# Output projection of three token blocks, head by head over both column halves, and Wo loaded in eight pieces

## The chip, the cores and the metric

The kernel runs on one core of a Trainium2 chip, as one launch. The metric is the device time of an execution in microseconds (us). Each kernel's time is the median of several executions; one more execution was recorded by the hardware profiler, and its trace is what the tables below come from.

## The reference

Two independent layers are computed on sequences of 2048 tokens of width 1024, and their outputs are set side by side. The first is a state-space layer (a complex diagonal recurrence over time with input and output matrices). The second, which the change concerns, is an attention with memory: 64 segments of 32 tokens, each preceded by 8 memory rows, 32 heads of width 128.

```python
for s in range(n_seg):
    xs = x[:, s * seg_len:(s + 1) * seg_len, :].copy()
    h = jnp.concatenate([mem, xs], axis=1)
    q, k, v = (jnp.einsum('btd,dhe->bhte', h, W) for W in (Wq, Wk, Wv))
    scores = jnp.where(mask, jnp.einsum('bhqe,bhke->bhqk', q, k) * scale, -1e9)
    o = jnp.einsum('bhqk,bhke->bhqe', softmax(scores), v)
    o = jnp.einsum('bhte,hed->btd', o, Wo)      # the output projection
    mem = o[:, :M, :].copy()
    outs.append(o[:, M:, :])
```

(Here the three projections and the mask are put on one line each.) The output projection is, for each token, a sum over 32 heads x 128 values against Wo, which has 1024 columns.

## The kernel before

**Stages.** Stage 1 interleaves the state-space layer's first products with the value projection. Stage 2 is the state-space output. Then come the query and key projections, interleaved with attention for 16 head pairs; the memory rows are guessed ahead, so that all segments run at once. The last stage is the output projection, with a range and tolerance check of the guess inside it (`check`). If the check fails, a flag sends the kernel into a slow general loop (`general`), which is not executed here.

**The output projection.** Attention stores its results in DRAM (`b_on`). Transposing DMAs on SP's queue bring them back as `ol[h]`, one tile of 128 (head width) x 512 tokens for each head; in the trace they are called b_ol. There are four blocks of 512 tokens (`tb`), each with four tiles of 128 tokens (`tt`). A matmul has 128 tokens of `ol[h]` as its stationary operand and 512 columns of Wo as the moving one. 32 such matmuls, one for each head, add up in one PSUM bank to a tile of 128 x 512. Wo lies in SBUF as two halves: `wo0` (columns 0 to 511; it takes over a buffer named t32, and the trace calls it t) and `wo1` (columns 512 to 1023; wo in the trace).

- `outproj_first` does block 0. Parts of it run between the last attention steps.
- `outproj` does blocks 1 to 3: for each `tt` and each half, 32 matmuls (`out_mm`) and then the eviction (`out_fin`): the vector engine (DVE) copies half 0 into the output tile b_ost, ScalarE (ACT) half 1, and SP stores the tile.
- `out_last` does the last tile of all in three parts of 512, 256 and 256 columns, each with its own copy and store, so that little is left behind the last matmul.

**PSUM.** Eight banks: three for tag "P" (trace: psP), two for "S" (psS), two for "O", one for "R" (psR). In blocks 1 to 3 before the change only "P" and, for the check, "R" are used.

**The check.** It is a generator of five steps. The first step loads b_omT; the other four are called by `next(ck, None)` each time `outproj` yields in block 2: two groups of 128 matmuls on psP (one for each half of Wo), a DVE reduction to c_ss, and last the flag. The flag step has two matmul groups on psR: the first sums c_ss over partitions, DVE then works out c_t, c_ok and c_bad from it, and the second (`ones` against c_bad) gives the flag, which DVE turns into an integer.

**Order.** A scheduler sets the order of instructions on each engine, except where `tc.keep_in_program_order` or the set `k.pin` holds it. With "PE" in `k.pin`, every call through `k.PE` keeps its program order; that is the case in stage 1 and 2 and, at the end, in block 3. `hint` places a branch hint on PE that must stand ahead of the branch to the general loop. DMA issues stand in their engine's queue (SP's for nearly all of the ones here) in order, and an issue that waits holds up those behind it.

Every matmul in this kernel is recorded through the same helper line (L69), so the profile is read by tile names.

Of the kernel before, what the change touches and what calls it, by code (L numbers as in the profile page):

```python
# [25 lines left out]
H = 32; E = 128; SEG = 32; M = 8; NSEG = 64; L = M + SEG  # L26
# [49 lines left out]
class K:  # L76
# [11 lines left out]
    def ps(self, tag, shape=(128, 512), dt=FP32):  # L88
        pool = self.psp if tag in "PR" else self.psx
        return pool.tile(list(shape), dt, name="ps" + tag, bufs={"P": 3, "S": 2, "R": 1, "O": 2, "U": 2}[tag])  # L90

    def copy(self, e, out, in_):
        if e == "s":
            self.S.activation(out, in_, ACT.Copy)  # L94
        else:
            self.V.tensor_copy(out, in_)  # L96
# [256 lines left out]
class PartB:  # L353
# [461 lines left out]
    def out_last(self, ol):  # L815

        k = self.k
        ot = self.p4a.tile([128, D], BF16, name="b_ost", bufs=4)
        for i, (c0, c1) in enumerate(((0, 512), (512, 768), (768, 1024))):
            p = k.ps("P")  # L820
            for h in range(H):
                k.PE.matmul(p[:, 0:c1 - c0], ol[h][:, 384:512], self.wo[c0 // 512][:, h, c0 % 512:c0 % 512 + c1 - c0], start=(h == 0), stop=(h == H - 1))
            k.copy("vsv"[i], ot[:, c0:c1], p[:, 0:c1 - c0])
            k.SP.dma_start(self.out[0, T - 128:T, D + c0:D + c1], ot[:, c0:c1])
            yield

    def outproj(self, tb, ol):
        k = self.k
        osts = {}
        for tt in range(4):  # L830
            if 4 * tb + tt == TT - 1:
                yield from self.out_last(ol)
                return
            for half in range(2):
                p = k.ps("P")
                self.out_mm(p, ol, tt, half, 0, H)
                self.out_fin(p, tb, tt, half, osts)
                yield


    def check(self):
# [166 lines left out]
def hint(k):  # L1008

    k.tc.mark_branch_hint_location("general", "LikelyTaken", engines=[mybir.EngineType.PE])  # L1010
    i = k.nc.cur_bb.bb.instructions[-1]
    k.tc.keep_in_program_order(type("Ins", (), {"ins": i}))


def kernel_main(tc, A_x, A_Lre, A_Lim, A_Bre, A_Bim, A_Cre, A_Cim, A_logdt, A_Dskip, B_x, B_mem0, B_Wq, B_Wk, B_Wv, B_Wo, out,
                force=False, dbg=None):
    with ExitStack() as ctx:
        k = K(tc, ctx)
# [3 lines left out]
        b = PartB(k, B_x, B_mem0, B_Wq, B_Wk, B_Wv, B_Wo, out)  # L1022

        def pool(name, side, bufs=2):
            return tc.tile_pool(name=name, bufs=bufs, side=side, reuse_waits="tile")
# [8 lines left out]
        with pool("p1x", "right") as p1x, pool("p1", "right", 1) as p1:  # L1034
# [29 lines left out]
            for kind, pc, q in order[1:]:  # L1064
# [3 lines left out]
                if kind == "v":  # L1068
                    b.v_x(pc, q, wv[pc])
                    if q == 3:  # L1070
                        if pc >= 3:
                            b.og(pc, wv[pc])
                        n = (pc + 2) if pc + 2 < PC else (2, 0)[pc + 2 - PC]
# [3 lines left out]
                n = 4 * pc + q  # L1077
# [27 lines left out]
        with pool("p2h", "right") as p2h, pool("p2", "right") as p2:  # L1105
# [5 lines left out]
            for i, _ in enumerate(s2):  # L1111
                if i in (1, 4, 7):
                    n = (2, 0, 1)[(i - 1) // 3]
# [25 lines left out]
        wo0 = t32.tile([128, H, 512], BF16, name="t32")  # L1139
# [6 lines left out]
        first, b.ol0 = None, []  # L1146
        for n, (hp, u) in enumerate(at):
            if n == 12:
                k.SP.dma_start(wo0[:], b.Wo[:, :, 0:512])
            if hp % 2 == 0 and 2 < hp + 2 < HP:  # L1150
                if u == 4:
                    vm = b.v_mem(hp // 2 + 1)
                if u in (4, 6, 8):
                    next(vm)
            if hp == 13 and u in (3, 6, 9):
                b.load_o_early(u // 3 - 1)
            want = min(18 * HP, LEAD + (n + 1) * 18 // 11)
            while done < want:
                next(pr)
                done += 1  # L1160
            if done == 18 * HP:
                if first is None:
                    xs.close()
                    b.p4a = ctx.enter_context(pool("p4a", "left", 1))
                    wo1 = b.p4a.tile([128, H, 512], BF16, name="wo1")
                    b.wo = (wo0, wo1)
                    b.load_o_early(3)
                    for h in range(0, H, 16):
                        k.SP.dma_start(wo1[:, h:h + 16, :], b.Wo[:, h:h + 16, 512:D])
                    first = b.outproj_first()  # L1170
                next(first)
                next(first)
# [2 lines left out]

        with pool("p4", "left") as p4:
            b.p4 = p4
            ol = b.load_o_all(1)
            for _ in first:
                pass  # L1180
            for tb in range(1, 4):
                nx = b.load_o_all(tb + 1) if tb < 3 else None
                if tb == 3:
                    k.pin.add("PE")
                if tb == 1:
                    ck = b.check()
                    next(ck)
                for n, _ in enumerate(b.outproj(tb, ol)):
                    if tb == 3 and n == 4:
                        hint(k)  # L1190
                    if tb == 2:
                        next(ck, None)
                ol = nx
# [9 lines left out]
@with_exitstack  # L1203
def kernel(
    ctx: ExitStack,
    tc: tile.TileContext,
    A_x: bass.AP,
    A_Lambda_re: bass.AP,
    A_Lambda_im: bass.AP,
    A_B_re: bass.AP,  # L1210
    A_B_im: bass.AP,
    A_C_re: bass.AP,
    A_C_im: bass.AP,
    A_log_dt: bass.AP,
    A_Dskip: bass.AP,
    B_x: bass.AP,
    B_mem0: bass.AP,
    B_Wq: bass.AP,
    B_Wk: bass.AP,
    B_Wv: bass.AP,  # L1220
    B_Wo: bass.AP,
    B_seg_len: bass.AP,
    out: bass.AP,
):
    assert int(B_seg_len) == SEG
    kernel_main(tc, A_x, A_Lambda_re, A_Lambda_im, A_B_re, A_B_im, A_C_re, A_C_im, A_log_dt, A_Dskip,
                B_x, B_mem0, B_Wq, B_Wk, B_Wv, B_Wo, out)
# [35 lines left out]
```

## Time and profile before

| | |
|---|---|
| time, median of 4 executions | 1238.62 us (1238.37 to 1238.72) |
| profiled execution: time / span | 1238.27 us / 1236.6 us |
| PE busy | 1229.9 us, 8174 matmuls and as many weight loads |
| DVE / ACT / POOL busy | 680.7 / 266.5 / 271.1 us |
| DMA | 174.20 MB, mean 141 GB/s |
| granted TensorE clock | 1.000 |
| blocks 1 to 3 of the output projection on PE | 1057.79 to 1232.35 us |
| last DVE copy | 1232.38 us, 0.42 us long |
| Wo issues on SP | first half at 511.00 us; second half at 999.89 and 1011.15 us |

The span runs from the first to the last recorded instruction; the execution's own time has 1.7 us more. "Busy" of PE counts matmuls with modelled ends: a matmul of 512 columns is shown as 0.38 us long, but the next one starts 0.216 us after it, so rows of a group are read from start to start. In the views below a line of the timeline has the start, the length of the group, engine, line, operation, output <- inputs, shape and count, and in square brackets the idle time before it with what ended it. In the list of waits a line has the waiter, what it waited for, the total, the number of times and the longest.

### The profile page before, as it was taken

How to read it: one execution, taken by the hardware profiler on the slowest of the kernel's cores; microseconds unless marked ns; L12 is line 12 of the kernel's file. 1: busy time of each engine (PE TensorE's matmuls, PEld its weight loads, DVE VectorE, ACT ScalarE, POOL GpSimd, SP SyncE). 2: the span in 40 equal slices, each digit the busy share in tenths (PEclk: the TensorE clock that was granted, in tenths of full speed). 3: DMA queues.
4: the chain of work that ended last, by engine and by line, in shares of the span. 5: the costliest groups of instructions: out<-in, count | busy, mean ns of one | idle time of the engine just before them, and what ended most of it. 6: DMA issues, size and time to landing. Idle time of an engine off the chain costs nothing.

```text
span 1236.6 us, 20043 instructions
## 1 busy us (share of the span) xinstructions
PE 1229.9 (99%) x8174; PEld 654.3 (53%) x8174; DVE 680.7 (55%) x1270; ACT 266.5 (22%) x694; POOL 271.1 (22%) x437
## 2 busy tenths in 40 slices
PE   9999999999999999999999999999999999999998
PEld 4444444444455555556666656555665554445444
DVE  4799999998711124666666666666666641001000
ACT  4444444443310000211112211111221110000000
POOL 4111232112322321322222222323222320000000
PEclk9999999999999999999999999999999999999999
DMA  9943455562898834855464645546574279507000
GB/s 243 249 148 93 126 142 141 155 171 88 232 301 265 248 120 95 228 132 139 96 154 109 153 109 130 131 91 132 116 151 96 61 208 241 108 17 154 18 17 27
DMA packets 321268, 174.20 MB, mean 141 GB/s; under 512 B 145882, under 2 KB 308876, under 8 KB 321172
## 3 DMA queue, kind: packets, MB, share of 16 engines
q1 hardware_dynamic: 299076, 145.33, 48.9%
q10 hardware_dynamic: 21072, 24.38, 6.0%
q0 software_dynamic: 1024, 3.17, 0.7%
q8 instruction: 65, 1.06, 0.4%
q14 instruction: 31, 0.25, 0.1%
HBM read 84.42 MB, written 53.96 MB: 112 GB/s over the span
## 4 chain that ended last, share of the span: by engine, by line
PE 98%; SPq 1%; DMA 0%; DVE 0%; issue 0%
PE psP L69 83%; PE psU L69 9%; PE psS L69 3%; PE psO L69 2%; PE psR L69 1%; SPq L69 1%; DMA b_wv<-in_B_Wv_dram 0%; DVE b_ost L96 0%
## 5 line engine op out<-in xcount | busy, mean ns | idle before, releaser
L69 PE MATMUL psP<-b_xe,b_wk 128*128 128x480 bf16 (+1 forms) x1280 | 247.5, 343 | 0.0
L69 PE MATMUL psP<-b_xe,b_wq 128*128 128x480 bf16 (+1 forms) x1280 | 247.5, 343 | 0.0
L69 PE MATMUL psP<-b_wv,b_xe 128*128 128x512 bf16 (+2 forms) x1048 | 224.5, 372 | 0.1
L689 POOL TENSOR_TENSOR b_m<-b_e,maskB 99x396 bf16<-99x396 bf16 (+1 forms) x160 | 134.4, 840 | 335.7 <-ACT b_e L688 335.7
L688 ACT ACTIVATE b_e<-psS 99x396 bf16<-99x396 f32 (+3 forms) x208 | 91.5, 442 | 530.4 <-PE psS L69 530.4
L69 PEld LDWEIGHTS <-b_wk 128*128 128x128 bf16 x1280 | 119.2, 98 | 94.2
L69 PEld LDWEIGHTS <-b_xe 128*128 128x128 bf16 x1056 | 101.8, 98 | 119.5 <-DMA b_xe<-in_B_x_dram 0.4
L69 PEld LDWEIGHTS <-b_wq 128*128 128x128 bf16 x1280 | 118.5, 98 | 87.7
L96 DVE CAST b_k<-psP 128x480 bf16<-128x480 f32 (+1 forms) x192 | 97.3, 528 | 100.0 <-PE psP L69 100.0
L96 DVE CAST b_q<-psP 128x480 bf16<-128x480 f32 (+1 forms) x192 | 97.3, 528 | 92.2 <-PE psP L69 90.9
L69 PEld LDWEIGHTS <-b_ol 128*128 128x128 bf16 x864 | 84.3, 98 | 94.4
L69 PE MATMUL psU<-a_xT,a_bt 128*128 128x512 bf16 x512 | 114.8, 379 | 0.0
L69 PE MATMUL psP<-t,a_hl 128*128 128x512 bf16 x512 | 113.1, 379 | 0.0
L96 DVE CAST b_ost<-psP 128x512 bf16<-128x512 f32 (+1 forms) x17 | 11.5, 676 | 177.6 <-PE psP L69 177.6
L69 PE MATMUL psP<-wo,b_ol 128*128 128x512 bf16 (+1 forms) x448 | 92.5, 364 | 0.0
L69 PE MATMUL psP<-t,b_ol 128*128 128x512 bf16 x416 | 92.2, 379 | 0.0
L94 ACT ACTIVATE b_vst<-psP 128x512 bf16<-128x512 f32 x126 | 72.3, 589 | 76.9 <-PE psP L69 72.8
L289 POOL TENSOR_SCALAR a_tt<-a_pr,a_tabf 128x1 f32<-128x1 f32 x48 | 34.6, 721 | 245.7 <-DVE a_pr L284 245.7
L706 DVE TENSOR_TENSOR b_ob<-psO,b_accR 99x384 bf16<-99x384 f32 x160 | 86.0, 554 | 2.9 <-DVE b_accR L705 0.4
L69 PEld LDWEIGHTS <-a_bt 128*128 128x128 bf16 x512 | 49.8, 98 | 59.5
L69 PEld LDWEIGHTS <-a_hl 128*128 128x128 bf16 x512 | 49.1, 98 | 56.6
L274 DVE TENSOR_TENSOR a_pr<-psU,a_tabf 128x2048 f32<-128x2048 f32 x32 | 73.1, 2284 | 9.2 <-PE psU L69 9.1
(203 smaller groups left out, 967.4 us busy)
## 6 DMA issues: line engine op xcount, KB each, us to landing
b_v<-b_vx SPq DMA_DIRECT2D x16, 1122.0 KB
b_wv<-in_B_Wv_dram SPq DMA_DIRECT2D x16, 1024.0 KB
b_vx<-b_vst ACTq DMA_DIRECT2D x24, 544.0 KB
b_on<-b_ob SPq DMA_DIRECT2D x15, 720.0 KB
a_hs<-a_h SPq DMA_DIRECT2D x32, 256.0 KB
b_wog<-in_B_Wo_dram SPq DMA_DIRECT2D x4, 2048.0 KB
b_wq<-in_B_Wq_dram SPq DMA_DIRECT2D x16, 512.0 KB
b_wk<-in_B_Wk_dram SPq DMA_DIRECT2D x16, 512.0 KB
```

The lines of the kernel that those rows point to most:

```text
L69: r = f(*a, **kw)
L94: self.S.activation(out, in_, ACT.Copy)
L96: self.V.tensor_copy(out, in_)
L274: V.tensor_tensor(pr[:], u[:].unsqueeze(1).to_broadcast([128, 2, 2, TB]), view(t3, [[TB + 1, 2], [TB + 1, 2], [1, TB]]), ALU.mult)
L289: G.tensor_scalar(tt[:, j:j + 1], w[:, j, TB - 1:TB], t3[:, 1, TB:TB + 1], None, ALU.mult)
L688: k.S.activation(e[:, a:b, :, 0:n], s[0:GW, a:b, :, 0:n], ACT.Exp, scale=float(E) ** -0.5, accum_out=self.accE[0:GW, j:j + 1])
L689: k.G.tensor_tensor(mv[:, a:b, :, 0:n], e[:, a:b, :, 0:n], mask[0:GW, :, 0:n].unsqueeze(2).to_broadcast([GW, b - a, 2, n]), ALU.mult)
L706: V.tensor_tensor(self.ob[:, b0:b0 + n, :], o[0:GW, 0:n, 0:E], r.unsqueeze(2).to_broadcast([GW, n, E]), ALU.mult)
```

## The change

1. `outproj` takes two PSUM banks at once for a tile of 128 tokens, "P" for even tiles and "S" for odd ones, and goes through the heads once: for each head the matmul with half 0 of Wo and then the one with half 1, both with the same stationary operand. Both evictions follow at the end of the tile, and the generator yields once for a tile instead of twice. So the check's four steps in block 2 come one for each tile.
2. A new helper, `again`, builds a matmul without a weight load of its own. It is defined and is not called.
3. "PE" is put into `k.pin` at the start of the last stage instead of at block 3.
4. `wo0` is loaded by four DMAs of eight heads each instead of one, `wo1` by four instead of two of sixteen heads.
5. In `out_last` the copy of the third part is split: ACT copies its second 128 columns and DVE its first.
6. The branch hint stands behind the third tile of block 3 instead of behind half 0 of that tile.

```diff
+    def again(self, out, w, x, start, stop):
+
+        PE = self.nc.tensor
+        i = mybir.InstMatmult(start_tensor_calc=start, stop_tensor_calc=stop, ldweights=False, name=self.nc.get_next_instruction_name(),
+                              engine=mybir.EngineType.PE, ins=[PE.lower_ap(x), PE.lower_ap(w)], outs=[PE.lower_ap(out)],
+                              tile_size=(128, 128), tile_position=(0, 0))
+        self.tc.keep_in_program_order(PE.add_instruction(i))
...
-            k.copy("vsv"[i], ot[:, c0:c1], p[:, 0:c1 - c0])
+            if i < 2:
+                k.copy("vs"[i], ot[:, c0:c1], p[:, 0:c1 - c0])
+            else:
+                k.copy("s", ot[:, c0 + 128:c1], p[:, 128:c1 - c0])
+                k.copy("v", ot[:, c0:c0 + 128], p[:, 0:128])
...
+            ps = [k.ps("PS"[tt % 2]) for _ in range(2)]
+            for h in range(H):
+                for half in range(2):
+                    k.PE.matmul(ps[half][:], ol[h][:, tt * 128:(tt + 1) * 128], self.wo[half][:, h, :], start=(h == 0), stop=(h == H - 1))
             for half in range(2):
-                p = k.ps("P")
-                self.out_mm(p, ol, tt, half, 0, H)
-                self.out_fin(p, tb, tt, half, osts)
-                yield
+                self.out_fin(ps[half], tb, tt, half, osts)
+            yield
...
             if n == 12:
-                k.SP.dma_start(wo0[:], b.Wo[:, :, 0:512])
+                for h in range(0, H, 8):
+                    k.SP.dma_start(wo0[:, h:h + 8, :], b.Wo[:, h:h + 8, 0:512])
...
-                    for h in range(0, H, 16):
-                        k.SP.dma_start(wo1[:, h:h + 16, :], b.Wo[:, h:h + 16, 512:D])
+                    for h in range(0, H, 8):
+                        k.SP.dma_start(wo1[:, h:h + 8, :], b.Wo[:, h:h + 8, 512:D])
...
             b.p4 = p4
+            k.pin.add("PE")
             ol = b.load_o_all(1)
...
-                if tb == 3:
-                    k.pin.add("PE")
...
-                    if tb == 3 and n == 4:
+                    if tb == 3 and n == 2:
                         hint(k)
```

## The prediction

> **What bounds the kernel now.** I read the page's engine table first, then its chain of waits, then who waited for whom on PE, then PE and DVE in order of time over the last 180 us, which is all that the change can reorder.
>
> ```profile
> PE 1229.9 (99%) x8174; PEld 654.3 (53%) x8174; DVE 680.7 (55%) x1270; ACT 266.5 (22%) x694; POOL 271.1 (22%) x437
> PEclk9999999999999999999999999999999999999999
> PE 98%; SPq 1%; DMA 0%; DVE 0%; issue 0%
> ```
>
> The kernel is one unbroken row of matmuls: PE is busy 1229.9 of 1236.6 us at the full granted clock, and 98% of the chain that ended last is PE. Each matmul has its own weight load (8174 and 8174), and the loads lie beside the matmuls. The list of waits on PE has two lines, both in the first microseconds:
>
> ```profile
> PE psR L69 <- DVE hpb L110: 1.3, 1, 1.3
> PE psU L69 <- DMA b_xr<-in_B_x_dram: 1.0, 1, 1.0
> ```
>
> So nothing that shortens a wait elsewhere can pay: only fewer or denser matmuls, a new hole in PE's row, or the few microseconds behind its last matmul move the end. PE in order of time, around the range check in token block 2:
>
> ```profile
> 1057.79 7.07 PE L69 MATMUL psP<-t,b_ol 128*128 128x512 bf16 x32
> 1064.70 7.07 PE L69 MATMUL psP<-wo,b_ol 128*128 128x512 bf16 x32
> ...
> 1119.95 4.22 PE L69 MATMUL psP<-b_omT,t 128*128 128x70 bf16 x128
> ...
> 1148.78 0.36 PE L69 MATMUL psR<-c_one,c_ss 128*70 128x1 f32 x4
> 1149.00 1.02 PE L69 MATMUL psP<-t,b_ol 128*128 128x512 bf16 x4
> 1149.97 0.17 PE L69 MATMUL psR<-c_bad,ones 128*1 128x3 bf16 x1
> 1150.07 6.22 PE L69 MATMUL psP<-t,b_ol 128*128 128x512 bf16 x28
> ...
> 1225.19 7.15 PE L69 MATMUL psP<-wo,b_ol 128*128 128x256 bf16 x64
> ```
>
> From start to start a group of 32 takes 6.91 us, 215.9 ns a matmul. The rows at 1148.78 to 1150.07 matter most: the check's two small matmul groups (psR) have a DVE chain between them, and the scheduler has put four projection matmuls into that gap. The chain itself, on DVE, with one eviction ahead of it:
>
> ```profile
> 1142.07 0.69 DVE L96 CAST b_ost<-psP 128x512 bf16<-128x512 f32 x1 [3.45 <-PE psP L69]
> 1149.17 0.15 DVE L875 COPY c_t<-psR 70x2 f32<-70x2 f32 x1 [6.41 <-PE psR L69]
> ...
> 1149.75 0.17 DVE L884 TENSOR_SCALAR c_bad<-c_ok 128x3 bf16<-128x3 f32 x1
> ```
>
> **1. The new matmul order: 0.** Eleven tiles of 128 tokens (four, four and three) each have 64 matmuls of 512 columns, before and after; 704 in all. Only the order changes: head by head, half 0 then half 1. In the built program each keeps its own weight load: 864 loads of b_ol stand in both programs, and the helper `again`, which would leave the load out, is called nowhere. So the second load of a pair repeats the first and none goes away.
>
> What could a repeated load save? 64 matmuls of 256 columns, less the last one's own 0.27 us, give (7.15 - 0.27) / 63 = 109.2 ns each; twice that less 215.9 is 2.5 ns, all that a matmul costs beyond its columns. So 352 repeats save at most 0.9 us and at least nothing. Can a repeat cost? The check's matmuls come every (4.22 - 0.20) / 127 = 31.7 ns, each with a new load of 98 ns, and PE has no hole there; a load inside 215.9 ns has far more room. I take 0, as no load is removed. The Trainium skill ("TensorE: Matmul & The Clock Gate", "Wait — 56ns, not 53.3ns?") puts the 2.5 ns behind decode, a fixed price per matmul; by it the saving would be nothing, where the rows leave up to 0.9 us.
>
> What could changing the accumulator bank at every matmul cost? The nearest rows are stage 1's, in groups of eight, where every eighth matmul changes bank (chain, in order of time):
>
> ```profile
> 97.84 6.91 PE psU L69 x32
> 104.75 6.91 PE psP L69 x32
> 111.66 3.45 PE psU L69 x16
> 115.11 6.91 PE psP L69 x32
> ```
>
> From 97.84 to 122.02 are 112 matmuls in 24.18 us with 14 changes; at the projection's pace (seven groups of 32 from 1064.70 to 1113.05, 215.85 ns each) 112 would be 24.175 us with 3.5. The rounding of the four times leaves -0.7 to +1.6 ns per change, so 704 changes cost -0.5 to +1.1 us. I take 0: the middle is half a nanosecond, and in attention the bank changes after three or four matmuls without a hole either. The same page ("A second HAM failure mode: psum-queue depth-cycling") speaks against this change: cycling through banks at 512 columns made the clock fall back to half in its kernel. By it 704 matmuls at half speed would add some 150 us (an estimate from the page); the rows above, at granted clock 1.00 with banks changing, show none of it.
>
> **2. The check on a pinned PE: +1.34 us.** PE is now held to program order from the start of the fourth pool instead of from block 3. In the built program the two psR groups stand directly behind one another, after the last tile of block 2; the four matmuls that filled the gap stand behind both. The waiting instruction is the weight load for the flag matmul (ones against c_bad), and all of block 3 is queued behind it. Moreover DVE now has an eviction in the way, since both halves of a tile end together. With T the end of the tile's row: half 0's last matmul starts at T - 0.43; an eviction starts 0.46 us after its last matmul starts (1064.95 against 1064.70 - 0.22), so at T + 0.03, and takes 0.69: T + 0.72. The first check group's result is there at T + 0.39 (1149.17 - 1148.78), so the eviction ends later, and the copy of c_t starts at T + 0.76 with the usual 0.04 between DVE instructions. From there to the flag matmul are 0.80 us (1149.97 - 1149.17), and 0.10 to the next projection matmul: T + 1.66. Before, the two groups took 0.22 + 0.10 = 0.32 us of PE. The difference is +1.34. Were DVE to take the eviction afterwards, it would be +0.97; were the chain hidden as before, 0. The check's two big groups move too (now after tiles 0 and 1), but their 2 x 4.05 us only change place, and the flag has over 50 us left.
>
> **3. The last copy in two parts: -0.10 us.** Behind PE's last matmul DVE copies 256 columns in 0.42 us (0.31 us after that matmul starts). By the slope from 512 columns (0.69) 128 columns are 0.29 on DVE; on ACT (0.60 and 0.38) 0.28, starting 0.05 later. The later of the two is ACT at 0.36 + 0.28 = 0.64 against 0.73. The output DMA waits for both. Bounds: -0.13 and 0.
>
> **4. Edits at nothing.** Wo in eight pieces: three more issues at 511 us and two more near 1000 to 1011 us, 0.4 to 0.6 us of SP each. SP is idle from 511.4 to 517.7 and from 1011.7 to 1015.8, which covers them; uncovered they would hold the stores of b_on and the loads of b_ol behind them by at most 1.2 us, and those are issued 20 us before PE needs them (1038 against 1057.8). The first piece of the second half is now 1 MB instead of 2, so the transpose behind it goes sooner; the rest lands by the time it did, with the same bytes; head 8 is first needed at 1030.16 + 8 x 0.216 = 1031.9. Banks: pairs alternate between psP and psS, so a pair is evicted (0.69 and 0.60 us side by side) 13.8 us before it is written again; were that cover gone it would be 0.7 us a tile. The branch hint stands 6.9 us later, behind which PE still has 13.8 us of matmuls; and PE's end has some 3 us of cover, as span 1236.6 ends 4.2 us after it.
>
> **Sum.** +1.34 - 0.10 = +1.24 us. The profiled execution took 1238.27 us (span 1236.6 and 1.7 around it), so 1239.5 by it; it lies 0.35 under the median of the four runs, 1238.62, from which the forecast is 1239.9 us. This kernel's measurement tells about 0.2%, 2.5 us, from no change, so this is "the same".
>
> **Rivals.** (a) *The repeat is cheap, or the check doesn't wait.* For: a pair shares its tile; the scheduler hid the chain before. Against: all the loads stand in the program, and PE's order is now fixed. It gives 1239.9 - 0.9 = 1239.0, or 1238.5 without the wait; all within 0.2%. That the change does less than its words say belongs here: no load goes. Chance 0.09.
> (b) *PE pays for changing bank at every matmul* (slower). The place is the 704 matmuls from 1057.8 on, the price x ns each. It decides from x = (2.48 - 1.24) / 704 = 1.8 ns; at 3 ns it is 1242.0, and if a matmul had to end before the next one began (379 ns long, 216 apart) 704 x 0.163 = 115 us more. For: no row alternates at every matmul. Against: the bound of 1.6 ns above. Chance 0.13, with what could go wrong in the load order.
> (c) *The pairs run denser than the columns allow* (faster by over 2.5 us): it needs 3.7 us from 704 matmuls, 5.3 ns each, twice the 2.5 ns there are. Only a lucky mix could. Chance 0.03.
> The forecast has the remaining 0.75.
>
> **How the numbers follow.** Same is 0.75 + 0.09 = 0.84, slower 0.13, faster 0.03. The range begins under (a)'s lower end, 1238.3, and goes up past the bank bound (1239.9 + 1.1) to (b) at 3 ns, 1242.0; beyond lie the larger prices of (b).
>
> **What would show it.** Right: projection matmuls 215.9 ns apart in pairs, 864 loads of b_ol, one new line among PE's waits of about 1.3 us for DVE c_bad near 1177 us, and no other hole; a tail shorter by 0.1. Wrong: spacing other than 215 to 217 ns (step 1), no such hole or one beyond 2 us (step 2), a wait of PE for Wo or b_ol (step 4).

## The result, and the profile after

The changed kernel takes 1239.92 us (median of 40 runs, 1239.47 to 1240.47) against 1238.39 us for the kernel before, measured beside it (60 runs): a ratio of 1.0012, with an interval from 1.0007 to 1.0016. That is 1.5 us slower, within the 0.2% that the forecast called the same, and 1239.9 was forecast. The profiled execution took 1239.83 us, its span is 1238.1 us; before it was 1238.27 and 1236.6. The total is right, but three of the terms under it are not, and their errors largely cancel.

The page of the kernel after, the lines that answer to those shown of before: PE has the same 8174 matmuls and weight loads and, within 0.1 us, the same busy time, and it carries the chain.

```profile
PE 1230.0 (99%) x8174; PEld 654.4 (53%) x8174; DVE 680.6 (55%) x1270; ACT 266.7 (22%) x695; POOL 271.1 (22%) x437
PE 98%; SPq 1%; DMA 0%; DVE 0%; issue 0%; ACT 0%
```

PE's waits have one new line, the one that step 2 named:

```profile
PE psR L69 <- DVE hpb L118: 1.3, 1, 1.3
PE psR L69 <- DVE c_bad L898: 1.0, 1, 1.0
PE psU L69 <- DMA b_xr<-in_B_x_dram: 0.8, 1, 0.8
```

The chain that ended last, in order of time (start, length, what), shows where the time goes. A tile's 64 matmuls, alternating banks at every one, take 13.81 us, as two groups of 32 did before (2 x 6.91). At 1176.41 the chain leaves PE for DVE, and it leaves it again at the end, where ACT and DVE follow one another:

```profile
1085.63 13.81 PE psP L69 x64
1099.44 13.81 PE psS L69 x64
...
1176.44 0.69 DVE b_ost L104
1177.13 0.07 DVE c_t L889
...
1177.84 0.17 PE psR L69
...
1233.48 0.29 ACT b_ost L102
1233.76 0.02 issue
1233.79 0.29 DVE b_ost L104
```

The next table cuts the end of each kernel into pieces, from the single instructions of its trace: from the first matmul of block 1 to the last matmul of all; from there to the issue of the last store; from the issue until SP sees the store's semaphore; and from there to the span's last instruction. In the last piece SP asks its eight queue semaphores one after the other, about 0.07 us each, and then the engines close. All numbers are starts, in us, from one profiled execution of each kernel. The first column says when block 1 starts.

| kernel | block 1 starts at | blocks 1 to 3 | to store's issue | to landing | to end | median of runs |
|---|---|---|---|---|---|---|
| before | 1057.79 | 174.28 | 0.76 | 1.67 | 2.02 | 1238.39 |
| after | 1057.84 | 175.33 | 0.94 | 2.24 | 1.66 | 1239.92 |
| e1 order only | 1057.78 | 175.32 | 0.76 | 1.70 | 2.02 | 1239.42 |
| e2 no early pin | 1057.88 | 175.33 | 0.94 | 2.21 | 1.66 | 1239.96 |
| e3 copy whole | 1057.94 | 175.33 | 0.76 | 1.69 | 1.66 | 1239.13 |
| e4 pin only | 1058.19 | 175.14 | 0.76 | 1.69 | 2.02 | 1239.36 |
| e5 flag step split | 1057.80 | 174.25 | 0.94 | 2.20 | 1.66 | 1238.80 |
| e6 both undone | 1057.71 | 174.25 | 0.76 | 1.72 | 1.66 | 1238.05 |
| e8 two banks | 1058.05 | 174.39 | 0.56 | 2.50 | 1.66 | 1238.86 |
| e9 Wo pieces only | 1057.72 | 174.27 | 0.76 | 1.73 | 1.66 | 1238.00 |
| e10 Wo in nine pieces | 1058.84 | 174.28 | 0.76 | 1.70 | 2.20 | 1239.53 |
| e11 late ACT | 1057.92 | 174.28 | 0.76 | 2.24 | 1.66 | 1238.63 |
| e12 copy split only | 1057.80 | 174.28 | 0.94 | 2.60 | 2.02 | 1239.41 |

After against before: +1.05 in the blocks, +0.18 to the issue, +0.58 to the landing, -0.36 to the end, and +0.05 in the start of block 1: +1.50, the 1.5 us between the spans.

### The profile page after: what moved, and what is told of

Same layout as the page of the kernel before. It is cut to its first block, busy times and chain, and to the rows that moved or that the text cites. A ratio compares the mean times of both kernels' runs of the same rounds, so it can differ in the third digit from the quotient of the medians.

```text
span 1238.1 us, 20047 instructions
## 1 busy us (share of the span) xinstructions
PE 1230.0 (99%) x8174; PEld 654.4 (53%) x8174; DVE 680.6 (55%) x1270; ACT 266.7 (22%) x695; POOL 271.1 (22%) x437
## 3 DMA queue, kind: packets, MB, share of 16 engines
q8 instruction: 65, 1.06, 0.4%
## 4 chain that ended last, share of the span: by engine, by line
PE 98%; SPq 1%; DMA 0%; DVE 0%; issue 0%; ACT 0%
PE psP L69 77%; PE psU L69 9%; PE psS L69 9%; PE psO L69 2%; PE psR L69 1%; SPq L69 1%; DMA b_wv<-in_B_Wv_dram 0%; DVE b_ost L104 0%; ACT b_ost L102 0%; DVE c_bad L898 0%; DVE c_ok L892 0%; DVE c_t L891 0%; DVE c_t L889 0%
## 5 line engine op out<-in xcount | busy, mean ns | idle before, releaser
L69 PE MATMUL psP<-wo,b_ol 128*128 128x512 bf16 (+1 forms) x288 | 87.5, 356 | 0.0
L69 PE MATMUL psP<-t,b_ol 128*128 128x512 bf16 x256 | 87.1, 379 | 0.0
L104 DVE CAST b_ost<-psP 128x512 bf16<-128x512 f32 (+1 forms) x12 | 7.9, 659 | 126.6 <-PE psP L69 120.0
```

Source lines behind the costliest of these rows:

```text
L69: r = f(*a, **kw)
```

## The experiments

Each was measured beside the kernel before. The ratios' intervals are about 0.0009 (1.1 us) wide on either side, so most contain 1; the medians stand in the table, and the pieces there decide. Apart from e4, e8 and e10, block 1 starts within 0.15 us of where it does in the kernel before; e4 and e8 start it later because PE stands still for 0.4 us at 15 us in their profiled executions, ahead of every edit.

**e5, flag step split.** In `check`, the step boundary behind the reduction is moved, so that a whole tile lies between the flag's two matmul groups:

```diff
             S.activation(sq[:, 0, cs, :], df[:], ACT.Square)
-            yield
+            if half == 0:
+                yield
...
+        yield
         pf = k.ps("R")
```

> The changed kernel, but the flag's second matmul group (ones against c_bad) stands one tile of 128 tokens behind the first, so that 64 projection matmuls lie between them. Theory (the loss is the hole in PE's row while DVE works out c_bad): PE's wait for c_bad is gone, the last matmul starts 1.05 us earlier than in the changed kernel, the time falls by about 1.05 us to some 1238.9. Rival (alternating the banks or repeating the weight load costs some 1.5 ns for each of 704 matmuls): the wait goes, but the last matmul starts as late as before the edit, within 0.1 us, and the time stays at 1239.9.

Ratio 1.0004 (0.9995 to 1.0013), 1.1 us under the changed kernel. The wait for c_bad is gone from PE's list, which holds only its two first lines again:

```profile
PE psR L69 <- DVE hpb L118: 1.3, 1, 1.3
PE psU L69 <- DMA b_xr<-in_B_x_dram: 1.2, 1, 1.2
```

The blocks take 174.25 us with the head-by-head order in place, 0.02 less than before the change. So neither the changing bank nor the repeated load costs anything that can be seen: over 704 matmuls it is less than 0.1 ns each. The rival of 1.5 ns a matmul is out.

**e4, pin only, and e1, order only.** Each is the kernel before with one of the two edits that could take the cover away:

```diff
 e4:         b.p4 = p4
+            k.pin.add("PE")
...
-                if tb == 3:
-                    k.pin.add("PE")
```

```diff
 e1: (in outproj, blocks 1 to 3; the hint at n == 2)
-            for half in range(2):
-                p = k.ps("P")
-                self.out_mm(p, ol, tt, half, 0, H)
...
+            for h in range(H):
+                for half in range(2):
+                    k.PE.matmul(ps[half][:], ...)
```

> The kernel before, with one edit: PE is held to program order from the start of the last stage. The flag step stands behind the second tile of block 2, half 1, whose eviction ACT does, so no DVE eviction is in the way. Theory: the two groups stand directly behind one another, the flag matmul waits 0.39 + 0.80 - 0.22 us, so the last matmul starts 0.87 us later than in the kernel before (1.29 us of PE for the two groups instead of 0.42), the time rises by 0.9 us. Rival (the pin alone costs nothing, the loss belongs to the head-by-head order): time as before within 0.2 us, no wait for c_bad.

> The kernel before, with one edit: blocks 1 to 3 take both halves of Wo head by head on alternating banks, one yield a tile (and the branch hint moved as in the change). No pin before block 3, Wo in three pieces, last copy whole. Theory: the flag's two groups come directly behind one another at the end of block 2, with block 3 pinned behind them, so the wait for c_bad is there as in the changed kernel (about 1.0 us), the last matmul starts 1.05 us later than in the kernel before; everything else is as before, time +1.05 us. Rival (only the pin takes the cover away): no wait, time as before.

e4: ratio 1.0008 (0.9998 to 1.0018), blocks +0.86 us where 0.87 was expected. e1: 1.0009 (0.9999 to 1.0018), blocks +1.05 us as expected. The line for c_bad among PE's waits, first e4, then e1:

```profile
PE psR L69 <- DVE c_bad L884: 0.8, 1, 0.8
```

```profile
PE psR L69 <- DVE c_bad L886: 1.0, 1, 1.0
```

Either edit alone brings the wait. With the order alone it is 0.19 us longer, because then DVE has half 0's eviction to do before it can turn to c_t: c_t starts 0.59 us behind the first psR matmul in e1 and 0.39 in e4.

**e2, no early pin.** The changed kernel, PE pinned only from block 3 as before.

```diff
             b.p4 = p4
-            k.pin.add("PE")
...
+                if tb == 3:
+                    k.pin.add("PE")
```

> The changed kernel, but PE is held to program order only from block 3 on, as before the change. Prediction's step 2 as worded (the pin at the start of the stage takes the cover away): the scheduler fills the gap again, PE's wait for c_bad is gone and the time is 1.05 us lower. Theory after reading the built program (the flag step now comes behind the last tile of block 2, and block 3, which is pinned in both, cannot be moved ahead of it): nothing changes, wait about 1.0 us, time 1239.9.

Ratio 1.0013 (1.0004 to 1.0022), every piece as in the changed kernel. The pin, which the prediction blamed, is not needed: the flag step has moved to the border of block 3, and what stands in that block may not pass it.

**e3, copy whole, and e6, both undone.** e3 is the changed kernel with the old line for the last copy; e6 has this and the edit of e5.

```diff
-            if i < 2:
-                k.copy("vs"[i], ot[:, c0:c1], p[:, 0:c1 - c0])
-            else:
-                k.copy("s", ot[:, c0 + 128:c1], p[:, 128:c1 - c0])
-                k.copy("v", ot[:, c0:c0 + 128], p[:, 0:128])
+            k.copy("vsv"[i], ot[:, c0:c1], p[:, 0:c1 - c0])
```

> The changed kernel, but the last 256 columns are copied by DVE in one piece, as before the change. Theory (the two half copies run one after the other, since both read one PSUM bank): from the start of the last matmul to the end of the last copy 0.73 us instead of 0.91, so 0.18 us less; wait for c_bad unchanged. Prediction's step 3 (the split gains 0.10): the time would rise by 0.10 us. Rival for the rest of the tail (the output DMA's landing is later because of the other order of queue semaphores, not because of the copy): issue of the last DMA to the end of the span stays at 3.95 us instead of falling to 3.74.

> The changed kernel with both edits: the flag's second group one tile later and the last copy in one piece. What is left of the change is the head-by-head order, the banks, the pin and Wo in eight pieces. Theory: these cost nothing, so the time is that of the kernel before within 0.3 us, and 1.2 us under the changed kernel. Rival (order, banks or Wo pieces cost something): 0.5 us or more above the kernel before.

e3: 1.0006 (0.9997 to 1.0015), 0.8 us under the changed kernel where 0.18 was expected. The issue comes 0.17 us sooner as expected; the store also lands 0.55 us faster, which nobody had expected, and the closing piece stays at 1.66, so this last difference is not the copy's. e6: 0.9998 (0.9989 to 1.0007), 0.34 us under the kernel before by the medians, so just outside the 0.3 expected, on the faster side. What is left of the change costs nothing. Two new questions: why does the store land later with the split copy, and where does the closing piece gain 0.36?

**e8, two banks.** e5 with the last 256 columns in two groups of 128, in a bank each.

```diff
+        pq = [k.ps("P"), k.ps("S")]
+        for h in range(H):
+            for j in range(2):
+                k.PE.matmul(pq[j][:, 0:128], ol[h][:, 384:512], self.wo[1][:, h, 256 + 128 * j:384 + 128 * j], ...)
+        for j in range(2):
+            k.copy("vs"[j], ot[:, 768 + 128 * j:896 + 128 * j], pq[j][:, 0:128])
```

> The changed kernel with the flag's second group one tile later, and the last 256 columns of the last tile computed as two groups of 128 columns in two PSUM banks, head by head; DVE copies one bank and ACT the other, into the same output tile. Theory (one shared PSUM bank is what made the two copies run one after the other): they run side by side, both start 0.3 to 0.36 us after the last matmul starts, and 0.64 us after it the later one ends, against 0.91 in the changed kernel; the matmuls take 64 x 55.8 instead of 32 x 109.2 ns, 0.08 us more. Time 1.05 + 0.27 - 0.08 = 1.24 us under the changed kernel. Rival (the copies are ordered because they write one output tile): DVE and ACT still one after the other, 0.91 us.

The last copy and the store's issue of the kernel before, then of the changed kernel, and then of e8, in order of time with what ended the idle time before:

```profile
1232.38 0.42 DVE L96 CAST b_ost<-psP 128x256 bf16<-128x256 f32 x1 [6.24 <-PE psP L69]
1232.83 0.33 SPq L69 DMA_DIRECT2D out_dram<-b_ost  x1
```

```profile
1233.48 0.28 ACT L102 ACTIVATE b_ost<-psP 128x128 bf16<-128x128 f32 x1 [3.06 <-PE psP L69]
1233.79 0.29 DVE L104 CAST b_ost<-psP 128x128 bf16<-128x128 f32 x1 [6.55 <-ACT b_ost L102]
1234.10 0.33 SPq L69 DMA_DIRECT2D out_dram<-b_ost  x1
```

```profile
1232.64 0.29 DVE L104 CAST b_ost<-psP 128x128 bf16<-128x128 f32 x1 [6.27 <-PE psP L69]
1232.69 0.28 ACT L102 ACTIVATE b_ost<-psS 128x128 bf16<-128x128 f32 x1 [3.14 <-PE psS L69]
1233.00 0.33 SPq L69 DMA_DIRECT2D out_dram<-b_ost  x1
```

In the changed kernel DVE was released by ACT; in e8 both by PE, side by side, though they write the same output tile. So it is the shared PSUM tile, one bank, that put the copies in a row; the wait itself is a semaphore in the program, which ACT's copy raises and DVE's waits for. The store is issued 0.38 us sooner, but the matmuls took 0.13 us more, the store 2.50 us to land, and the median is that of e5: the expected 1239.92 - 1.24 = 1238.7 against 1238.86 measured, with a ratio of 1.0005 (0.9995 to 1.0014).

**e11, late ACT.** e6, plus a one-column ACT copy from another bank that nobody uses.

```diff
+                if i == 2 and h == H - 4:
+                    pr = k.ps("R")
+                    k.PE.matmul(pr[:, 0:1], ol[h][:, 384:512], self.wo[1][:, h, 0:1], start=True, stop=True)
+                    late = self.p4a.tile([128, 1], BF16, name="late", bufs=1)
+                    k.copy("s", late[:], pr[:, 0:1])
```

> The changed kernel with the flag's second group one tile later and the last copy whole (as in the run with both undone), plus one small ACT copy of one column from another PSUM bank, whose matmul stands four matmuls before the last; its result is used by nothing. So ACT reaches the branch at the end as late as with the split copy, while the last copy (DVE, 0.42 us) and the store's issue stay at 0.76 us behind the start of the last matmul. Theory (an instruction transfer of 8 KB, fetched for ACT when it gets to its branch, falls on the store's packets): the store lands about 0.4 to 0.5 us later, 2.1 to 2.2 us behind its issue instead of 1.7, and the end 4.5 to 4.6 us behind the last matmul instead of 4.14. Rival (the store is slower because two engines wrote its tile, or since two copies in a row delay it): 1.7 and 4.14 us.

```profile
1232.16 0.17 ACT L102 ACTIVATE late<-psR 128x1 bf16<-128x1 f32 x1 [2.74 <-PE psR L69]
```

The store, untouched and issued at the same 0.76, takes 2.24 us instead of 1.72 to land, and the end moves to 4.66 us behind the last matmul (4.14 in e6); median +0.58 over e6, ratio to before 1.0002 (0.9993 to 1.0011). So a late ACT alone delays the store. In all seven kernels where ACT's last work is the second part's copy the store lands in 1.67 to 1.73 us; in all six where ACT has work behind PE's last few matmuls it takes 2.20 to 2.60. The list of DMA queues, between 1233.5 and 1236 us, first before, then after (q14 is a queue that the profile marks as carrying instructions):

```profile
q14 instruction: 2, 0.02, 2.0%
```

```profile
q14 instruction: 3, 0.02, 3.8%
```

Each of these transfers is one packet of 8 KB and takes 0.3 to 0.7 us. In the kernel before the two start at 1234.19 and 1234.53, behind the end of the store's last packet (1234.02); after, the first runs from 1235.13 to 1235.63, between the store's packets, the last of which ends at 1235.83. The trace doesn't name the engine that a transfer is for, but in all thirteen traces one starts 1.1 to 1.5 us behind ACT's closing branch: 2.0 to 2.2 us ahead of the store's issue where ACT is done early, 0.8 to 1.5 us behind the issue where it is not. So I take the third one to be ACT's.

The packets show what it delays. The store has 144, which makes nine for each of the core's 16 DMA engines. In the changed kernel 135 have ended 1.18 us behind the issue; the other nine end one after the other from 1.55 to 1.72 us, right behind the end of the first transfer (1.53). Of the 16 updates of the store's semaphore 15 come by 1.58 us and the last at 2.23. The other five kernels with a late ACT have nine such packets too, from 1.49 us on; the seven with an early one have none, with every packet ended by 1.19 us. The Trainium skill ("DMA: Bandwidth & Descriptors", "Queues, rings and completion order") says that a DMA engine works off a whole packet of one queue before it turns to another, which would make the store's packets on that engine wait for the 8 KB; nine late packets, one engine's share, agree with it, though the trace doesn't say which engine moved them.

**e12, copy split only.** The kernel before with the split copy, the reverse of e3's diff.

> The kernel before, with one edit: the last copy split between ACT and DVE as in the change. Theory: the copies run one after the other (0.91 us behind the start of the last matmul instead of 0.73), the store takes about 0.5 us longer, so the end is 0.65 to 0.7 us later than 4.45, time +0.7 us. Prediction's step 3: 0.10 us less, 4.35. Matmuls as before.

Ratio 1.0008 (0.9998 to 1.0017). The copies in a row are there (0.94 to the issue), but the store takes 0.94 us longer, not 0.5, and the end is 1.1 us later, median +0.97. The direction is the theory's, the size is not. Here the three 8 KB transfers start within 0.33 us of one another, the first of them 1.43 us behind the issue instead of 1.02, and the nine late packets follow its end, from 1.76 to 1.97 us. Why it starts later, and so how much a store loses, stays open.

**e9 and e10, Wo in pieces.** The kernel before with Wo in eight pieces as in the change (e9), and in nine (e10).

```diff
 e9:
-                k.SP.dma_start(wo0[:], b.Wo[:, :, 0:512])
+                for h in range(0, H, 8):
+                    k.SP.dma_start(wo0[:, h:h + 8, :], b.Wo[:, h:h + 8, 0:512])
...
-                    for h in range(0, H, 16):
-                        k.SP.dma_start(wo1[:, h:h + 16, :], b.Wo[:, h:h + 16, 512:D])
+                    for h in range(0, H, 8):
+                        k.SP.dma_start(wo1[:, h:h + 8, :], b.Wo[:, h:h + 8, 512:D])
 e10: range(0, H, 4) with h + 4 for wo0, range(0, H, 32) with h + 32 for wo1
```

> The kernel before, with one edit: Wo in eight pieces as in the change. Theory (five more DMAs turn the round of eight queue semaphores by five, so the last store posts to the semaphore that SP asks for last in its closing list instead of third; the five other questions then lie beside the store instead of behind it): matmuls of blocks 1 to 3 as before within 0.03 us, from the start of the last matmul to the end of the span 4.13 us instead of 4.45, so 0.3 us less. Prediction's step 4 (nothing): 4.45. Rival (the shorter end in the runs without the split copy comes from the PE order or the pin): 4.45.

> The kernel before, with one edit: the first half of Wo in eight pieces of four heads and the second in one, six more DMAs than before in place of five. Theory (the place in the closing list decides): the last store posts to the semaphore that SP asks for first, seven questions of about 0.07 us come behind its landing, and the end takes 4.45 + 2 x 0.08 = 4.6 us behind the start of the last matmul. Rival (smaller pieces as such, less in the queues at the end): 4.1 us as with eight pieces.

e9: 0.9997 (0.9988 to 1.0006). The interval takes in 1, but all its 11 runs (1237.89 to 1238.12) lie under all 33 of before that were measured beside it (1238.19 to 1238.72); the lowest of the 60 in the result is 1238.07. The closing piece is 1.66 us as expected. e10: 2.20, as expected too. The DMAs take the eight semaphores in turn, and SP asks them in a fixed order at the end. Posted to the one asked third (before), the last store has five questions behind it; asked last (five DMAs more), none; asked first (six more), seven. That is all that the pieces of Wo do for the time, and it is an accident of their number. e10 as a whole is 1.1 us slower (ratio 1.0009, 1.0000 to 1.0018), most of it for another reason, which I had not expected: it starts block 1 1.05 us later. The transpose of the last quarter of block 0's b_ol stands behind the one large piece of Wo's second half in SP's queue (its issue takes 16.48 us), and PE waits for it:

```profile
PE psP L69 <- DMA b_ol<-b_on: 0.8, 1, 0.8
```

e9 and e6 are the fastest kernels here, 0.3 to 0.4 us under the one before by their medians; with these intervals that is not told from no change.

## Why the prediction was right, and where it was not

**Step 1, the matmul order at 0: right.** 13.81 / 64 = 215.8 ns a matmul, 864 loads of b_ol, and e5 and e6 show nothing left in the blocks. The granted clock stays at 1.00 through them. The section of the Trainium skill that step 1 weighed ("TensorE: Matmul & The Clock Gate", "A second HAM failure mode: psum-queue depth-cycling") tells of a kernel in which PE stood idle for short times between groups of matmuls while it went through the banks. Here tile follows tile without such a gap, 13.81 us each, and changing the bank at every matmul did nothing to the clock.

**Step 2, the check, +1.34 forecast, +1.05 measured: the mechanism right, the size too large, the reason half right.** Two terms were mis-sized: when DVE gets to c_t, and what the two groups had cost before. The groups around the flag:

```profile
1176.44 0.69 DVE L104 CAST b_ost<-psS 128x512 bf16<-128x512 f32 x1 [13.12 <-PE psS L69]
1176.45 0.36 PE L69 MATMUL psR<-c_one,c_ss 128*70 128x1 f32 x4
1177.05 0.15 DVE L889 COPY c_t<-psR 70x2 f32<-70x2 f32 x1
1177.61 0.17 DVE L898 TENSOR_SCALAR c_bad<-c_ok 128x3 bf16<-128x3 f32 x1
1177.84 0.17 PE L69 MATMUL psR<-c_bad,ones 128*1 128x3 bf16 x1 [1.03 <-DVE c_bad L898]
1177.93 0.39 PE L69 MATMUL psP<-t,b_ol 128*128 128x512 bf16 x1
```

With T at 1176.45 the eviction starts at T - 0.01, not T + 0.03, and c_t at T + 0.60, not T + 0.76: its recorded start even lies before the eviction's recorded end. So the next projection matmul comes at T + 1.48, not T + 1.66. And the two groups had cost 0.42 us of PE before, not 0.32: between the end of the four filling matmuls (1149.00 + 4 x 0.216 = 1149.86) and the flag matmul (1149.97) lay 0.10 us that I had not counted. 1.48 - 0.42 = 1.06. The reason given, the pin, is enough by itself (e4), but not needed (e2): the step's new place at the border of block 3 does it too (e1).

**Step 3, the split copy, -0.10 forecast: wrong.** The step that failed is "the later of the two is ACT": it took the two copies as lying side by side. They read one bank and run in a row, +0.18 us. The Trainium skill ("PSUM — Partial Sum Buffer", "PSUM bank collisions raise a hardware error") says that two engines must be kept apart by bank and quadrant, which speaks against this part of the change. e8 agrees in so far as with two banks the wait is gone (0.05 us between the two starts); what two engines on one bank at once would do, no run here shows. On top comes a cost that no step had: ACT works to the very end, and the store lands 0.58 us later (0.52 in e11 against e6).

**Step 4, edits at nothing: the cover holds, a price and the sum don't.** The four issues of Wo's first half took SP 5.97 us, not 0.4 to 0.6 each: one after the other 0.37, 0.80, 1.39 and 3.27 us. Why they grow isn't shown; the semaphore that the last one waits for had its last update at 510.38, before that issue began at 513.15. But they ended at 516.42, in the idle time that the step named, and the store behind them started at 517.78 (517.73 before). SP's queue before, and then after:

```profile
511.00 0.37 SPq L69 DMA_DIRECT2D t<-in_B_Wo_dram  x1
517.73 8.32 SPq L69 DMA_DIRECT2D b_on<-b_ob  x2
...
1000.39 10.71 SPq L69 DMA_TRANSPOSE b_ol<-b_on  x1
1011.15 0.57 SPq L69 DMA_DIRECT2D wo<-in_B_Wo_dram  x1
```

```profile
510.45 5.97 SPq L69 DMA_DIRECT2D t<-in_B_Wo_dram  x4
517.78 8.00 SPq L69 DMA_DIRECT2D b_on<-b_ob  x2
...
1000.44 6.83 SPq L69 DMA_TRANSPOSE b_ol<-b_on  x1
1007.32 3.51 SPq L69 DMA_DIRECT2D wo<-in_B_Wo_dram  x3
```

The transpose behind the first piece left SP at 1007.3 instead of 1011.1, sooner, as step 4 said. What it did not see is the turn of the semaphores: -0.36 us (e9). Banks and hint cost nothing.

**The sum.** Forecast +1.34 - 0.10 = +1.24; measured +1.05 + 0.18 + 0.58 - 0.36 + 0.05 = +1.50. That the forecast of 1239.9 met 1239.92 is partly luck: errors of -0.3 (step 2), +0.9 (step 3) and -0.4 us (step 4) largely cancel, and of the 0.3 us by which the change costs more than forecast, 0.2 is made up by the kernel before, which is that much lower in 60 runs than in the four that I started from. Of the rivals, (a) is out, as the wait is there and a repeated load saves nothing; (b) and (c) are out by 13.81 us a tile. Whether a pair without its second load would run denser was not tried: `again` is called nowhere, and no run leaves a load out.

## What to carry to other kernels

Where PE has no holes, ask of a change only what stands between two dependent matmuls and what lies behind the last one. A small chain through another engine (here 1.4 us for a flag) is free only while independent matmuls stand inside it; a change of loop, of yields or of pins can push them out, and moving the second half of the step one tile on brings them back. At the end of a kernel count more than the last copy: which bank the copies share, which engine works last, and which semaphore the last store posts to made 0.2 to 0.6 us each in the changed kernel.

## What the runs showed of the hardware, unexpected

- ACT kept busy to the end delays the last store, even where ACT has nothing to do with it (e11): landing 1.67 to 1.73 us in seven kernels with ACT done early, 2.20 to 2.60 in six with ACT late, by nine of the store's 144 packets.
- The closing of the program takes 1.66, 2.02 or 2.20 us behind the last store's landing, as its semaphore is the last, the third or the first that SP asks for; the values repeat within 0.01 us in all kernels.
- On DVE the next instruction can have its recorded start 0.08 us before the recorded end of the one ahead of it (1177.05 against 1176.44 + 0.69).
